# An attention and MLP block on one core: four maxima moved ahead, and K's loads, the last spare copies and a row of ones moved in the DMA queue

## The chip, the core and the metric

The kernel runs on one core of a Trainium2 chip. The core has a matrix engine (TensorE, PE in the profile, with its weight loads as PEld), a vector engine (VectorE, DVE), a scalar engine (ScalarE, ACT), a general engine (GpSimd, POOL) and a queue engine (SyncE, SP) that here issues nearly all DMAs. Each engine works through its own list of instructions in order and waits on semaphores for the others.

The metric is the device time of one execution in microseconds. Before the change it is 1146.16 us, the median of three runs (1145.81 to 1146.93).

## What is computed

One transformer block over 2048 tokens of width 448, with 16 heads of 28 columns. A conditioning vector `c` gives six modulation rows. The part that matters here is the attention, with its softmax over all 2048 keys:

```python
def _A_ref(x, wqkv, wo):
    B, S, D = x.shape
    H = 16; Dh = D // H
    qkv = (x @ wqkv).reshape(B, S, 3, H, Dh).transpose(2, 0, 3, 1, 4)
    q, k, v = qkv[0], qkv[1], qkv[2]
    scale = Dh ** -0.5
    scores = jnp.einsum("bhqd,bhkd->bhqk", q, k) * scale
    p = _softmax(scores, axis=-1)
    o = jnp.einsum("bhqk,bhkd->bhqd", p, v)
    return o.transpose(0, 2, 1, 3).reshape(B, S, D) @ wo
...
h = _layernorm(x) * (1 + ca) + sa
x = x + ga * _A_ref(h, A_wqkv, A_wo)
h = _layernorm(x) * (1 + cb) + sb
x = x + gb * _B_ref(h, B_w1, B_b1, B_w2, B_b2)
```

`_B_ref` is a second layer norm, a product with `w1`, a GELU and a product with `w2`.

## The kernel before

**Stages.** Phase 1 takes the tokens in four blocks of 512 (`b` = 0 to 3) and makes Q, K and V. Q and K are kept as a rounded high part and a low rest (`hi`, `lo`), four heads to a group (`g` = 0 to 3). `qk_task` and `v_task` are the tasks of a block; `n` counts them. Phase 2 is the attention in 16 units (a group times a block of queries) of 16 steps, and phase 3 is the MLP.

**Maxima.** The softmax needs the largest score of each query row before phase 2 can use that query block. For every group, query block, key block and head a small product (`L464`) writes 128x512 scores into a PSUM bank and VectorE reduces them to 128 maxima (`L469`). Some are done as a pair for two key blocks: ScalarE takes the positive part of the difference (`L477`) and VectorE adds and reduces in one operation (`L481`). A pair is two small products, one ScalarE and one VectorE operation; two single maxima are two products and two VectorE operations. All of them go through a ring of five PSUM banks (`ma` twice, `m2` twice, `m1`) plus the bank `o` for a sixth one. The maxima are spread over the tasks: `emit_task` puts five or six products behind each task's own product, and `emit_mid` puts four single ones into its middle. Before the change `emit_mid` is used in tasks 1, 3, 5 and 7 of block 1 alone. What is left for group 0 and query block 0 at the end of phase 1 is done by `finish_max(0, 0)`.

**The road into phase 2.** `max_fin` gathers the finished maxima of a query block (`L500`), and two tasks later `put` transposes them (`L507`) and stores them with four small DMAs (`L510`) as row 28 of each head in `slot_b`, the query tile. The first product of phase 2 (`L1155`) reads 29 rows of `slot_b` and of the key tile `slot_a`, so it waits for the four `L510`, for Q's loads and for K's loads (`L651`). K's loads of a block's 2x4 tiles go into the slots that held the weights, and read Q's and K's parts back from DRAM (`d`), where each `qk_task`'s split has stored them (`L432`, 256 KB each).

**SP's queue.** SP issues its DMAs in the order of the code. They take turns on eight semaphores, so each of them also waits until the DMA eight places before it has landed; the listing of waits shows that for every row of the queue.

- `put_spare` (`L369`) copies four heads' spare rows from DRAM to DRAM for the Q or K task before; it reads what the two `L432` of that task have written.
- `put_ones` (`L357`) writes a row of ones into a K tensor. Its source is a part of `slot_d0`. The exponentials of the first step of phase 2 (`L1160`) write into that same slot, so the first of them waits until the last `L357` has been read out.
- `L492` loads a finished group's next `hi` part, `L834` loads rows of the output weight `wo`.

In block 3, tasks 0 to 4 are Q1, K1, Q2, K2, Q3 (the last Q), and tasks 5 to 7 are V.

Of the kernel before, what the change touches and what calls it, by code (L numbers as in the profile page):

```python
# [39 lines left out]
def tile_adaln_block(ctx: ExitStack, tc: tile.TileContext, x, wqkv, wo, w1, b1, w2, b2, c, w_mod, out):  # L40
# [29 lines left out]
    def nm(t):  # L70
        uid[0] += 1
        return f"{t}_{uid[0]}"
# [22 lines left out]
    def ps_s():  # L95
        return ps_tile("pa", 2)
# [11 lines left out]
    def f(t):  # L108
        return t.bitcast(F32)
# [226 lines left out]
    def v_init(i):  # L336
        pool.memset(v_sb[i][:, :, :, DH : DH + 1], 1.0)
        pool.memset(v_sb[i][:, :, :, DH + 1 : 32], 0.0)
# [11 lines left out]
    def by_head(t):  # L350
        return t.rearrange("(j r) n -> j r n", r=32)
# [4 lines left out]
    def put_ones(g):  # L356
        sp.dma_start(  # L357
            f(dscr[1][0][g])[DH:128:32, :].rearrange("j (q r) -> j q r", r=256),
            ones[:, None, :].broadcast_to([4, 8, 256]),
        )  # L360
# [4 lines left out]
    def put_spare():  # L365
        for kind, g, sl in spare:
            n = 4 * (4 * kind + g)
            for part in range(2):
                sp.dma_start(  # L369
                    by_head(f(dscr[1][part][3]))[:, n : n + 4, sl], by_head(f(dscr[kind][part][g]))[:, DH:32, sl],  # L370
                )
        spare.clear()
# [65 lines left out]
    def v_task(b, t, p):  # L438
        ts = slice(t * 128, (t + 1) * 128)
        hh, hl = hT[b]  # L440
        mm_acc(p[:, :D], terms448(
            lambda k: hh(k)[:, ts], lambda k: hl(k)[:, ts], lambda k: wv[0][:, k, :], lambda k: wv[1][:, k, :],
        ), p1_n[3] if phase1[0] else None)
        if phase1[0]:
            emit_task(*p1_n[:3])
        act.copy(v_sb[b][:, t, :, :DH], p[:, :D].rearrange("p (h d) -> p h d", d=DH))
# [41 lines left out]
    def load_hi(kind, g, b):  # L488
        tg = ("kh" if kind else "qh") + str(b)
        t = sb.tile([128, 512], F32R, tag=tg, name=nm(tg), bufs=1)  # L490
        (kh_sb if kind else qh_sb)[(g, b)] = t
        sp.dma_start(f(t), f(dscr[kind][0][g])[:, b * 512 : (b + 1) * 512])  # L492
# [113 lines left out]
    p1_n = [0, False, 1, None]  # L606
# [41 lines left out]
    def load_parts(tag, kind, g, sl):  # L648
        t = slot(tag, [128, 2, 512])
        for part in range(2):  # L650
            sp.dma_start(f(t)[:, part, :], f(dscr[kind][part][g])[:, sl])  # L651
        return t

    def load_k(g, ch):
        kst[(g, ch)] = load_parts(f"a{ch}", 1, g, slice(ch * 512, (ch + 1) * 512))
# [37 lines left out]
    for b in range(NB):  # L693
        more = b + 1 < NB
        tasks = []
        for g in range(1 if b else 0, NG):
            tasks += [(b, 0, g), (b, 1, g)][: 2 if g + 1 < NG else 1]
        if b == 0:
            tasks[1], tasks[2] = tasks[2], tasks[1]

        tasks += [(b, 2, t) for t in range(4 if more else 3)]
        if more:
            stages, later = stages[-4:] if b else stages, ln1_stages(b + 2) if b + 2 < NB else None
            xs_next = []
            tasks += [(b + 1, 0, 0), (b + 1, 1, 0)]
        for n, (tb, kind, g) in enumerate(tasks):
            post = []
            ready, newq = newq, []
            if not more and n == len(tasks) - 2:

                mx_ring[:] = ["ma", "ma", "m2", "m2", "m1"]
            p1_n[0] = P1RATE if b < 1 else P1RATE + 1
            if not more and n == len(tasks) - 1:
                p1_n[0] = 0

            k = n - (6, 4, 4, 4)[b]
            p1_n[1] = not (more and (0 <= k < NC)) and not (b == 1 and n < 4)
            p1_n[2] = (3 if n > 3 else 1) if b == 3 else 2 if b == 2 and p1_n[1] else 1
            p1_n[3] = emit_mid if b == 1 and n in (1, 3, 5, 7) else None
            if kind < 2:  # L720
                fn = qk_task(tb, kind, g, firsts[n] if b == 0 and n < 3 else None)
                if g == 0:
                    fn()
                else:
                    post.append(fn)
                if kind == 1 and (g == 0 or (g == 1 and tb < 2)):
                    newq = [(g, qt, cch) for qt in range(tb + 1) for cch in range(tb + 1) if max(qt, cch) == tb]
            else:
                v_task(tb, g, ps_s())
            for item in ready:  # L730
                queue_max(*item)
            if b == 0 and 2 <= n < 6:
                prep_w(2, n - 2, act.copy, dve)
            if more:
                k = n - (6, 4, 4, 4)[b]

                if b == 0 and n in (0, 1, 3, 4):
                    x = 2 * n if n < 2 else 2 * n - 2
                    for fn in stages[x : x + 2]:
                        fn(xs_next)  # L740
                if b and n < 4:
                    stages[n](xs_next)
                if 0 <= k < NC:
                    post.append(h_chunk(b + 1, xs_next, k))
                if later and 7 <= n < 11:
                    later[n - 7](None)
            if n == (4 if b else 6):
                v_init(b)
            if b == 0 and n == 6:
                mod_load(0)  # L750
                mod_load(1)
            if b == 1 and n == 8:
                put_last_rows()
            if b == 2 and n == 5:
                sp.dma_start(b1_col, b1.rearrange("(k p) -> p k", p=128))
            if b == 1:
                if n < 2:
                    mod_mm(n)
                    mod_load(2 + n)
                elif n in (2, 3):  # L760
                    mod_mm(n)
                    if n == 3:
                        mod_fin()
            if not more:
                if n == 0:
                    load_q(0)
                    load_q(1)
                if n == 6:
                    put_spare()
                if n in (2, 4, 6):  # L770
                    put_ones(n // 2 - 1)
                if n == 5:
                    act.activation(cols[:, 0:1], zero_col, AF.Exp)
                    for ch in range(4):
                        load_k(0, ch)
            tick_late()
            for fn in post:
                fn()
        if more:
            stages = later  # L780
# [21 lines left out]
    phase1[0] = False  # L802
    for item in deferred:
        load_hi(*item)
    for g in range(1, NG):
        for qt in range(NB):
            for cch in range(NB):
                queue_max(g, qt, cch)
# [323 lines left out]
    for u in range(NU):  # L1132
        g, qt = divmod(u, NB)
        for kt in range(NKT):
# [10 lines left out]
            n = n_maxima(step)  # L1145
# [81 lines left out]
    for n in range(len(seq) + LAG):  # L1227
        if n < len(seq):
            b, i = seq[n]
# [53 lines left out]
```

## Time and profile before

| what | value |
|---|---|
| median of three runs | 1146.16 us |
| the profiled execution, its own time | 1145.55 us |
| its span from first to last instruction | 1143.8 us |
| granted TensorE clock, mean | 0.995 |
| PE busy in the span | 98% |
| phase 1 (PE's last product of it ends) | 167.5 us |
| phase 2's first product starts | 176.8 us |

The 1.75 us between the span and the execution's own time lie around the program. The times inside the trace are counted from the start of the span. "Idle before" in a row is time in which that engine did nothing, with the instruction or the DMA whose end let it go on.

### The profile page before, as it was taken

What the parts mean: (1) busy time and instruction counts of PE and PEld (TensorE: products, weight loads), DVE (VectorE), ACT (ScalarE), POOL (GpSimd) and SP (SyncE); (2) the same over time, 40 slices, a digit from 0 to 9 for tenths busy, and PEclk for the clock granted to TensorE, in tenths of its full rate; (3) what the DMA queues carried; (4) which work ended last, traced back from release to release, by engine and by line L of the source; (5) the groups of instructions that cost most, each with busy time, mean ns of one, the idle gap of its engine ahead of it and who ended that gap; (6) DMA issues with size and microseconds to landing.
All of it is one profiled execution on the core that took longest, in us unless ns stands there. A gap on an engine that the chain in (4) does not pass through costs nothing.

```text
span 1143.8 us, 20663 instructions
## 1 busy us (share of the span) xinstructions
PE 1125.3 (98%) x8319; PEld 674.9 (59%) x8319; DVE 832.2 (73%) x1485; ACT 672.3 (59%) x825; POOL 209.6 (18%) x211
## 2 busy tenths in 40 slices
PE   9999988999999999999999999999999999999998
PEld 6756764444444444444444444545458888888887
DVE  6968776999989999998999877586438853444322
ACT  4555755877877787877788777576862321211110
POOL 1533331210000000000000011207114503123000
PEclk9999998999999999999999999999999999999999
DMA  8562362111231211221211222020423100000000
GB/s 300 201 209 76 103 215 66 47 57 57 66 99 53 56 49 38 66 85 57 58 48 55 74 80 74 13 84 1 128 59 89 43 33 1 1 33 1 33 1 33
DMA packets 49389, 81.16 MB, mean 71 GB/s; under 512 B 12307, under 2 KB 18762, under 8 KB 49294
## 3 DMA queue, kind: packets, MB, share of 16 engines
q1 hardware_dynamic: 48810, 79.11, 21.9%
q8 instruction: 65, 1.06, 0.4%
q10 hardware_dynamic: 148, 0.46, 0.1%
q0 software_dynamic: 336, 0.28, 0.1%
q14 instruction: 30, 0.25, 0.1%
HBM read 54.94 MB, written 26.45 MB: 71 GB/s over the span
## 4 chain that ended last, share of the span: by engine, by line
PE 93%; DVE 3%; DMA 2%; issue 1%; ACT 1%; SPq 0%; POOL 0%; DVEq 0%; ACTq 0%; POOLq 0%
PE s L1155 27%; PE o L1125 21%; PE m L386 16%; PE pa L386 8%; PE m L464 6%; PE s L1218 4%; PE s L1219 4%; PE s L1217 4%; DVE mxp L469 2%; PE o L267 1%; PE m L267 1%; DMA slot_a<-d 1%; PE ma L464 0%; DMA osb<-drec 0%; DMA slot_d<-in_c_dram 0%
## 5 line engine op out<-in xcount | busy, mean ns | idle before, releaser
L469 DVE TENSOR_REDUCE mxp<-m 128x1 f32<-128x512 f32 x879 | 555.0, 684 | 97.4 <-PE m L464 94.3
L1155 PE MATMUL s<-slot_b,slot_a 28*128 28x512 f32 (+1 forms) x3072 | 384.8, 424 | 9.5 <-DMA slot_b<-full 9.2
L1160 ACT ACTIVATE slot_c<-s 128x1024 f32<-128x1024 f32 x340 | 329.6, 1022 | 82.5 <-PE s L1155 81.7
L1155 PEld LDWEIGHTS s<-slot_b,slot_a 28*128 28x128 f32 (+1 forms) x3072 | 216.9, 184 | 259.8 <-ACT slot_c L1160 148.9
L464 PE MATMUL m<-kh,qh 28*128 28x512 f32 x867 | 289.5, 472 | 0.5 <-DVE mxp L469 0.2
L1160 ACT ACTIVATE slot_d<-s 128x1024 f32<-128x1024 f32 x172 | 166.8, 1022 | 52.6 <-PE s L1155 41.4
L1125 PE MATMUL o<-slot_c,v 128*32 128x512 f32 x1360 | 181.2, 605 | 0.0
L1201 ACT ACTIVATE full<-m,b_col 128x512 f32<-128x512 f32 x56 | 38.5, 688 | 191.9 <-PE m L386 179.7
L1204 DVE CAST hi<-full 128x512 fp32r<-128x512 f32 x56 | 25.2, 450 | 135.2 <-ACT full L1201 135.2
L464 PEld LDWEIGHTS m<-kh,qh 28*128 28x128 f32 x867 | 115.0, 182 | 8.5 <-DVE mxp L469 4.8
L891 POOL TENSOR_TENSOR osb<-osb,osb 128x512 f32<-128x512 f32 x16 | 21.1, 1316 | 449.7 <-DMA osb<-drec 321.4
L1125 PE MATMUL o<-slot_d,v 128*32 128x512 f32 x688 | 92.5, 605 | 0.4 <-ACT osb L1094 0.4
L386 PE MATMUL m<-y,slot_a 128*128 128x512 f32 x160 | 60.6, 395 | 0.0
L1125 PEld LDWEIGHTS o<-slot_c,v 128*32 128x32 f32 x1360 | 26.8, 108 | 53.7 <-issue 53.3
L1205 DVE TENSOR_TENSOR lo<-full,hi 128x512 fp32r<-128x512 f32 x56 | 44.1, 788 | 5.2
L386 PE MATMUL m<-y,slot_c 128*128 128x512 f32 x152 | 47.5, 396 | 0.1
L1219 PE MATMUL s<-slot_v,lo 128*128 128x448 f32 x128 | 46.7, 365 | 0.0
L1217 PE MATMUL s<-slot_v,hi 128*128 128x448 f32 x128 | 46.6, 364 | 0.0
L469 DVE TENSOR_REDUCE mxp<-ma 128x1 f32<-128x512 f32 x56 | 36.7, 682 | 10.1 <-PE m L464 5.1
L386 PE MATMUL m<-y,slot_v 128*128 128x512 f32 x112 | 39.2, 396 | 0.0
L386 PE MATMUL m<-y,slot_b 128*128 128x512 f32 x112 | 39.0, 397 | 0.0
L477 ACT ACTIVATE slot_d<-m 128x512 f32<-128x512 f32 x33 | 18.7, 596 | 28.5 <-PE m L464 14.9
(249 smaller groups left out, 1412.1 us busy)
## 6 DMA issues: line engine op xcount, KB each, us to landing
slot_b<-d SPq DMA_DIRECT2D x32, 256.0 KB
slot_a<-d SPq DMA_DIRECT2D x32, 256.0 KB
d<-lo SPq DMA_DIRECT2D x28, 256.0 KB
d<-hi SPq DMA_DIRECT2D x16, 256.0 KB
osb<-drec SPq DMA_DIRECT2D x15, 256.0 KB
out_dram<-xn SPq DMA_DIRECT2D x16, 224.0 KB
raw<-in_B_w_dram SPq DMA_DIRECT2D x14, 224.0 KB
qh<-d SPq DMA_DIRECT2D x12, 256.0 KB
```

The lines of the kernel that those rows point to most:

```text
L386: pe.matmul(p, a, b, start=(i == 0), stop=(i == len(terms) - 1))
L464: pe.matmul(m, qh_sb[(g, qt)][js, i * 128 : (i + 1) * 128], k[js, :], start=True, stop=True)
L469: dve.tensor_reduce(out=mxp[(g, qt)][:, i, j, cch : cch + 1], in_=m, op=ALU.max, axis=AX.X)
L1125: pe.matmul(o[32 * j : 32 * j + 32, :], v_sb[kt // 4][:, kt % 4, 4 * g + j, :], p[:, j, :], start=(kt == 0), stop=(kt == NKT - 1),)
L1155: pe.matmul(s2[:, jj, :], ks[rows_, kp, kc], qs[rows_, qp, :], start=(term == 0), stop=(term == 2))
L1160: act.activation(pt[:, 2 * hf : 2 * hf + 2, :], s2, AF.Exp, scale=SCALE)
L1201: act.activation(gf, p, AF.Gelu_apprx_tanh, bias=b1_col[:, i : i + 1])
L1204: dve.tensor_copy(ghi, gf)
L1205: dve.tensor_tensor(out=glo, in0=gf, in1=f(ghi), op=ALU.subtract)
L1217: pe.matmul(pp, ghi[:, ts], w_hi, start=(m == 0), stop=False)
L1218: pe.matmul(pp, ghi[:, ts], w_lo, start=False, stop=False)
L1219: pe.matmul(pp, glo[:, ts], w_hi, start=False, stop=(m == NFT - 1))
```

## The change

Five edits, all of them in phase 1:

1. Task 8 of block 2, the last V task of that block, now has `emit_mid` in its middle: four single maxima.
2. In block 3 the tasks with three pairs begin at task 5 and no longer at task 4. Task 4 has one pair and four single maxima, as tasks 0 to 3 have.
3. K's eight loads are issued in task 4, ahead of that task's split, and no longer in task 5.
4. The last spare copies (`put_spare` of Q3) and the third row of ones (`put_ones(2)`) are issued behind phase 1, after the deferred `L492`, and no longer in task 6.
5. With edits 1 and 2 no maximum is left for `finish_max(0, 0)`; the gathering of query block 0 comes in task 4 and its store in task 5.

```diff
             p1_n[1] = not (more and (0 <= k < NC)) and not (b == 1 and n < 4)
-            p1_n[2] = (3 if n > 3 else 1) if b == 3 else 2 if b == 2 and p1_n[1] else 1
-            p1_n[3] = emit_mid if b == 1 and n in (1, 3, 5, 7) else None
+            p1_n[2] = (3 if n > 4 else 1) if b == 3 else 2 if b == 2 and p1_n[1] else 1
+            p1_n[3] = emit_mid if (b, n) in ((1, 1), (1, 3), (1, 5), (1, 7), (2, 8)) else None
...
                 if n == 0:
                     load_q(0)
                     load_q(1)
-                if n == 6:
-                    put_spare()
-                if n in (2, 4, 6):
-                    put_ones(n // 2 - 1)
+                if n == 4:
+                    for ch in range(4):
+                        load_k(0, ch)
                 if n == 5:
                     act.activation(cols[:, 0:1], zero_col, AF.Exp)
-                    for ch in range(4):
-                        load_k(0, ch)
+                if n in (2, 4):
+                    put_ones(n // 2 - 1)
...
     for item in deferred:
         load_hi(*item)
+    put_spare()
+    put_ones(2)
```

The order of the instructions shows the moves at two places. The first is SP's queue. Before, from Q2's spare copies to the first of K's loads; `d003` and `d013` are Q3's two parts in DRAM, `slot_a0` is the first key tile:

```order
L369 DMA d103_240<-d002_231 4x4x512
L369 DMA d113_244<-d012_235 4x4x512
L357 DMA d101_238<-slot_d0_4_86 4x8x256
L432 DMA d003_232<-hi_453_1905 128x512
L432 DMA d013_236<-lo_455_1907 128x512
L369 DMA d103_240<-d102_239 4x4x512
L369 DMA d113_244<-d112_243 4x4x512
L651 DMA slot_a0_463_1950<-d100_237 128x512
```

and from the last of K's loads on:

```order
L651 DMA slot_a3_466_1959<-d110_241 128x512
L369 DMA d103_240<-d003_232 4x4x512
L369 DMA d113_244<-d013_236 4x4x512
L357 DMA d102_239<-slot_d0_4_86 4x8x256
L510 DMA slot_b0_413_1740<-full_480_2024 4x4x32 x4
L492 DMA qh0_481_2038<-d001_230 128x512
L834 DMA raw_495_2097<-in_A_wo_dram 28x448 x4
```

K's first load now stands right behind Q2's two spare copies. From the last of K's loads on, the changed queue reads:

```order
L651 DMA slot_a3_464_1935<-d110_241 128x512
L357 DMA d101_238<-slot_d0_4_86 4x8x256
L432 DMA d003_232<-hi_458_1920 128x512
L432 DMA d013_236<-lo_460_1922 128x512
L369 DMA d103_240<-d102_239 4x4x512
L369 DMA d113_244<-d112_243 4x4x512
L510 DMA slot_b0_417_1752<-full_472_1977 4x4x32 x4
L492 DMA qh0_481_2035<-d001_230 128x512
L369 DMA d103_240<-d003_232 4x4x512
L369 DMA d113_244<-d013_236 4x4x512
L357 DMA d102_239<-slot_d0_4_86 4x8x256
L835 DMA raw_495_2097<-in_A_wo_dram 28x448 x4
```

Five DMAs that stood ahead of K's loads now stand between them and the maxima's four stores, and the last three small ones stand behind those stores.

The second place is PE in task 8 of block 2, the second half of its own product (`pa_376`) and the maxima behind it. Before:

```order
L386 MATMUL pa_376_1595<-slot_e1_21_126,slot_b0_221_970 128x448
L386 MATMUL pa_376_1595<-slot_e0_20_125,slot_b1_222_971 128x448 x2
L386 MATMUL pa_376_1595<-slot_e0_20_125,slot_b1h_223_972 128x448
L386 MATMUL pa_376_1595<-slot_e1_21_126,slot_b0_221_970 128x448
L386 MATMUL pa_376_1595<-slot_e0_20_125,slot_b0_221_970 128x448
L464 MATMUL m2_377_1607<-raw_159_726,qh2_276_1196 128x512
L464 MATMUL m1_378_1610<-raw_159_726,qh2_276_1196 128x512
L464 MATMUL ma_379_1613<-raw_178_806,osb_161_745 128x512
L464 MATMUL ma_380_1616<-raw_178_806,osb_161_745 128x512
L464 MATMUL m2_381_1619<-kh0_70_355,qh2_276_1196 128x512
L464 MATMUL o_382_1622<-kh0_70_355,qh2_276_1196 128x512
```

and in the changed kernel, from the first of the four new maxima on:

```order
L464 MATMUL m2_377_1601<-raw_178_806,osb_161_745 128x512
L464 MATMUL m1_378_1604<-raw_178_806,osb_161_745 128x512
L464 MATMUL ma_379_1607<-raw_178_806,osb_161_745 128x512
L464 MATMUL ma_380_1610<-raw_178_806,osb_161_745 128x512
L386 MATMUL pa_376_1595<-slot_e1_21_126,slot_b0_221_970 128x448
L386 MATMUL pa_376_1595<-slot_e0_20_125,slot_b1_222_971 128x448 x2
L386 MATMUL pa_376_1595<-slot_e0_20_125,slot_b1h_223_972 128x448
L386 MATMUL pa_376_1595<-slot_e1_21_126,slot_b0_221_970 128x448
L386 MATMUL pa_376_1595<-slot_e0_20_125,slot_b0_221_970 128x448
L464 MATMUL m2_381_1619<-raw_159_726,qh2_276_1196 128x512
L464 MATMUL m2_382_1622<-raw_159_726,qh2_276_1196 128x512
L464 MATMUL m1_383_1625<-raw_178_806,osb_161_745 128x512
```

Four of the five banks are now taken ahead of the second half, and the six maxima behind it go through the same banks once more. The numbers of PE's and VectorE's instructions in the whole program are the same in both kernels; ScalarE has two fewer.

## The prediction

> **What bounds the kernel now.** I read the page's busy times and its chain first, then the list of waits, then the timeline around the one long wait.
>
> ```profile
> span 1143.8 us, 20663 instructions
> PE 1125.3 (98%) x8319; PEld 674.9 (59%) x8319; DVE 832.2 (73%) x1485; ACT 672.3 (59%) x825; POOL 209.6 (18%) x211
> PE 93%; DVE 3%; DMA 2%; issue 1%; ACT 1%; SPq 0%; POOL 0%; DVEq 0%; ACTq 0%; POOLq 0%
> PE s L1155 <- DMA slot_b<-full: 9.2, 1, 9.2
> ```
>
> PE is busy nearly always and carries 93% of the chain. It has one wait of any size: 9.2 us, once, in which the first product of phase 2 waits for the maxima's store (`L510`, `slot_b<-full`). PE's timeline and its windows show the place:
>
> ```profile
> 166.84 0.72 PE L464 MATMUL m<-kh,qh 28*128 28x512 f32 x2
> ...
> 176.80 0.79 PE L1155 MATMUL s<-slot_b,slot_a 29*128 29x512 f32 x2 [9.24 <-DMA slot_b<-full]
> ...
> core 0: us, PE busy (x) PEld busy (x) DVE busy (x) ACT busy (x) POOL busy (x), PEclk, DMA share, GB/s
> 167.50:176.80 9.30, 0.06 (x1) 0.03 (x1) 2.78 (x6) 0.00 (x0) 0.00 (x0) 0.66 0.73 229
> 176.80:180.00 3.20, 3.20 (x18) 2.37 (x19) 2.36 (x4) 1.46 (x2) 0.45 (x1) 0.50 0.58 165
> ```
>
> Phase 1 ends at 167.56 and phase 2 begins at 176.80. All that the change can win lies in this gap, since the same products, in the same number, stand before and behind it. So I compute one moment: when the last of the four `L510` lands. It landed at 176.56, by the chain and SP's timeline:
>
> ```profile
> 160.42 1.29 SPq L369 DMA_DIRECT2D d<-d  x2
> 161.76 0.46 SPq L357 DMA_DIRECT2D d<-slot_d  x1
> 162.27 0.34 SPq L432 DMA_DIRECT2D d<-hi  x1
> 162.66 0.78 SPq L432 DMA_DIRECT2D d<-lo  x1
> 163.54 1.23 SPq L369 DMA_DIRECT2D d<-d  x2
> 164.81 4.66 SPq L651 DMA_DIRECT2D slot_a<-d  x8
> 169.51 1.67 SPq L369 DMA_DIRECT2D d<-d  x2
> 171.57 0.27 SPq L357 DMA_DIRECT2D d<-slot_d  x1
> 172.29 2.46 SPq L510 DMA_DIRECT2D slot_b<-full  x4
> 174.91 0.34 SPq L492 DMA_DIRECT2D qh<-d  x1
> ...
> 168.32 5.89 DMA slot_a<-d
> 174.23 2.33 DMA slot_b<-full
> ...
> SPq L510 <- DMA slot_a<-d: 0.4, 1, 0.4
> ```
>
> K's first load is issued at 164.81. The chain runs through one of K's loads, which lands at 174.21, to the last `L510`, whose turn on the eight semaphores it held, and 2.33 us later that has landed: 11.75 us from K's first issue. The gathering of the maxima isn't on this road: the stores wait for K's loads.
>
> **The change part by part, on that road.**
>
> *Four maxima in the middle of block 2's task 8.* The trace has this edit already in block 1, whose V tasks 6 and 7 are alike but for `emit_mid` in task 7:
>
> ```profile
> 83.39:86.87 3.48, 3.48 (x22) 2.68 (x21) 2.02 (x6) 1.53 (x3) 1.21 (x1) 1.00 0.76 292
> 86.87:92.17 5.30, 5.12 (x25) 3.21 (x24) 5.30 (x10) 3.21 (x6) 1.35 (x2) 1.00 0.21 32
> 130.81:134.26 3.45, 3.45 (x22) 2.67 (x21) 2.46 (x6) 2.32 (x5) 1.22 (x2) 1.00 0.00 0
> ...
> 90.98 1.28 DVE L469 TENSOR_REDUCE mxp<-m 128x1 f32<-128x512 f32 x2
> ...
> 91.11 0.49 PE L464 MATMUL ma<-kh,qh 28*128 28x512 f32 x1
> 91.75 0.50 PE L464 MATMUL m<-raw,osb 28*128 28x512 f32 x1
> ```
>
> Task 6 takes 3.48 us, task 7 5.30: 1.82 more. In task 7 VectorE is busy throughout, and PE's last two maxima start at 91.11 and 91.75, each right after VectorE has left its bank. Task 8 of block 2 (130.81 to 134.26) has no middle maxima yet. There too VectorE's 2.46 us are the maxima that the task before has left to it, and the fourth and fifth maxima behind it need the banks of the third and fourth middle ones. I take +1.82. The lower end is the bare products, from a middle whose banks were free:
>
> ```profile
> 60.34 0.51 PE L464 MATMUL m<-kh,qh 28*128 28x512 f32 x3
> 60.35 0.49 PE L464 MATMUL ma<-kh,qh 28*128 28x512 f32 x1
> 60.78 0.50 PE L386 MATMUL pa<-slot_c,slot_a3h 128*128 128x512 f32 x1
> ```
>
> 60.34 to 60.78 is 0.44. The upper end is VectorE's full time, four operations at half of two in 1.28 us, or 0.64 each: 2.56. What comes later in phase 1, SP's stores and loads too, hangs on these tasks and moves by the same amount.
>
> *K's loads.* Their first issue moves from 164.81 to the end of Q2's spare copies, 160.42 + 1.29 = 161.71, the start of the `L357` that it displaces at 161.76: -3.05 us. Q3's product, whose weights lie in K's slots, must be done by then, and it is; its maxima already run at
>
> ```profile
> 157.81 0.39 PE L464 MATMUL ma<-kh,qh 28*128 28x512 f32 x1
> ```
>
> The ends are -2.65, if SP waits once for a landing as the stores did (0.4), and -3.39, if the first load, with less ahead of it, comes in half a piece of 256 KB sooner (0.34, by the rate below).
>
> *What now stands between K's loads and the stores.* Before: two spare copies and a row of ones. Now the same three small ones and, new, Q3's two writes of 256 KB. The nearest price for such a piece is the rate at which K's own loads came in:
>
> ```profile
> 171.00:173.00 2.00, 0.00 (x0) 0.00 (x0) 0.00 (x0) 0.00 (x0) 0.00 (x0) 0.50 1.04 388
> ...
> 146.27 1.85 SPq L651 DMA_DIRECT2D slot_b<-d  x4
> 148.22 0.37 SPq L432 DMA_DIRECT2D d<-hi  x1
> ...
> 154.64 1.28 SPq L369 DMA_DIRECT2D d<-d  x2
> ```
>
> 262,144 bytes at 388 GB/s are 0.68 us, two are 1.35. That they would be paid is seen after Q's loads: the write issued at 148.22 behind four loads let the spare copy that reads it go only at 154.64, 6.4 us later, so pieces come through in the order of issue. The lower end is +0.55: the last store must at least wait until K's eighth load and the ones have landed instead of the seventh. The upper end is +1.65, with the small copies drawn out by 0.3 besides. I take +1.15, nearer the upper end because of that last row; part of the writes runs while the stores still wait for their turn.
>
> [...]
>
> *What is off the road.* The four maxima at the end of phase 1 (166.84, 0.72 us) go, but 9 us of waiting follow them: 0. Task 4 of block 3 gets five VectorE operations in place of three, and ScalarE two fewer. Tasks 0 to 3 have just these five:
>
> ```profile
> 144.41:147.80 3.39, 3.39 (x19) 2.46 (x17) 3.07 (x7) 1.67 (x4) 1.36 (x2) 1.00 0.45 158
> ```
>
> VectorE needs 3.07 of 3.39 us, so PE isn't held; a stall of some tenths in the shorter V task behind it ends in the gap too: 0. The store of the maxima is ready two tasks sooner, and waits for K's loads as before: 0. The last spare copies and ones behind the stores shift the loads of `wo` by about 2 us; they feed POOL, which no one waits for there: 0. The last `L357` holds back ScalarE's first exponential, whose cover is this:
>
> ```profile
> 178.54 1.94 ACT L1160 ACTIVATE slot_d<-s 128x1024 f32<-128x1024 f32 x2 [11.06 <-DMA raw<-in_A_wo_dram]
> ...
> 182.62 0.39 PE L1155 MATMUL s<-slot_b,slot_a 29*128 29x512 f32 x2
> ```
>
> PE comes back to that bank at about 182.4, behind the last V product. An exponential takes half of 1.94, so it may start as late as 181.4, 2.8 us later than now. With the stores issued at about 174.5 the `L357` follows after an `L492` (0.34), two spare copies (1.67), 0.4 of waiting and its own 0.27, at 177.2; with 2.33 to land that is 179.5: 0.
>
> *The sum.* +1.82 - 3.05 + 1.15 = -0.08. The gap shrinks at its front, to about 8 us, but its end stays: PE begins phase 2 at about 176.7. PE's clock was 0.50 in the first 3.2 us behind the gap, and I leave that as it is. The profiled execution took 1145.55 us (1143.8 and 1.75 around it), so 1145.5 by this sum. The median of the runs shown is 0.61 above that execution, so 1146.1.
>
> **The rivals.**
>
> *Faster: the lead is kept.* Block 2's task 8 finds its banks free (0.44), the writes are hidden behind the turns of the stores (0.55), and K's loads come in sooner (-3.39): -2.40, 1143.8. For it: block 2's tasks leave VectorE idle for 1 us each (2.46 of 3.45). Against it: block 1's task 6 leaves still more (2.02 of 3.48) and task 7 paid all the same. With one of the three alone it stays within 0.2%.
>
> *Slower: the ones come too late.* Place: ScalarE's first exponential behind the last `L357`. It decides from 181.4 on; from there each microsecond costs one. It is now the last of thirteen DMAs behind K's loads, where each waits for the one eight before. For it: two `L369` took 1.67 us to issue for their waits alone. Against it: 1.9 us of cover beyond my 179.5. At 184.0 it would give +2.6, 1148.7.
>
> *The change doesn't do what it says: K's loads don't go sooner.* If SP, at 161.76, still waits for landings and goes only where it went before, the lead is 0: +1.82 + 1.15 = +2.97, 1149.1; half the lead gives 1147.6. For it: SP waited at 154.64 for a write. Against it: SP went on at once, from 161.71 to 161.76, and K's first load waits for PE alone.
>
> **How the numbers follow.** The likeliest is the sum, 1146.1, with 0.58; its own range is 1144.4 to 1147.6: the middle at 0.44 alone gives -1.46, at 2.56 alone +0.66, and the runs shown lie from 0.35 below to 0.77 above their median. The kept lead has 0.18 (0.12 of it beyond 0.2%), the late ones 0.12 (0.08 beyond), the lost lead 0.12 (0.05 beyond). A difference of 0.2%, 2.3 us, is about what a measurement of this kernel can tell from no change: faster 0.12, same 0.75, slower 0.13. With a tenth left out on either side the range is 1144.0 to 1148.2.
>
> **What the changed profile would show.** Block 2's task 8 lasts about 5.3 us, and VectorE is busy through it (or 3.9, if the lead is kept). K's first load is issued near 163.6 and the last `L510` near 174.5. PE's one wait is still for `slot_b<-full`, about 8 us, and ends near 176.7; the first exponential starts before 180. If PE begins phase 2 before 175 or after 178.5, or waits for an exponential in the first two steps, the prediction is wrong; so it is if phase 2 itself is no longer as long as before.

## The result, and the profile after

The changed kernel takes 1146.44 us, the median of 12 runs (1145.59 to 1148.41); the kernel before took 1146.23 us beside it (12 runs, 1144.25 to 1148.56). The ratio is 1.0001, with a 95% interval of 0.9992 to 1.0010: no change that can be measured. The profiled execution took 1146.05 us, with a span of 1144.3. Two lines of the page, and the first of PE's list of waits:

```profile
span 1144.3 us, 20654 instructions
PE 1126.0 (98%) x8319; PEld 675.0 (59%) x8319; DVE 833.1 (73%) x1485; ACT 671.4 (59%) x823; POOL 209.8 (18%) x211
```

```profile
PE s L1156 <- DMA d<-d: 7.7, 1, 7.7
```

PE's one long wait has shrunk from 9.2 to 7.7 us. It is put down to a spare copy (`d<-d`), which the product doesn't read: that copy was landing when the wait ended, and the last `L510` had landed 0.35 us before. SP's queue after the change:

```profile
162.66 3.95 SPq L651 DMA_DIRECT2D slot_a<-d  x8
166.66 0.68 SPq L357 DMA_DIRECT2D d<-slot_d  x1
167.44 0.40 SPq L432 DMA_DIRECT2D d<-hi  x1
169.37 0.32 SPq L432 DMA_DIRECT2D d<-lo  x1
169.97 1.23 SPq L369 DMA_DIRECT2D d<-d  x2
171.33 2.62 SPq L510 DMA_DIRECT2D slot_b<-full  x4
```

In this execution all of phase 1 ran 0.92 us earlier than in the profile before, from the program's start on. So I count places from the first product of block 2's task 8, which stands at 131.22 in the profile before and at 130.30 here. K's first load moved from +33.6 to +32.4, and phase 2's start from +45.6 to +45.9. PE's timeline at that start, the first product that sums values (`o<-slot_d,v`), and ScalarE's first exponential:

```profile
176.17 0.80 PE L1156 MATMUL s<-slot_b,slot_a 29*128 29x512 f32 x2 [7.72 <-DMA d<-d]
...
178.50 4.17 PE L386 MATMUL m<-slot_e,slot_c 128*128 128x448 f32 x11
...
185.15 1.06 PE L1126 MATMUL o<-slot_d,v 128*32 128x512 f32 x8
```

```profile
178.69 1.94 ACT L1161 ACTIVATE slot_d<-s 128x1024 f32<-128x1024 f32 x2 [9.67 <-DMA raw<-in_A_wo_dram]
```

In the windows (start and end, length, PE's busy time, granted clock, DMA share, GB/s) of both kernels the gap reads like this, before first:

```profile
167.11:170.52 3.41, 0.45 (x4) 1.00 0.88 242
170.52:173.93 3.41, 0.00 (x0) 0.50 0.87 327
173.93:177.35 3.42, 0.55 (x4) 0.50 0.42 105
177.35:180.76 3.41, 3.41 (x20) 0.50 0.45 123
180.76:184.17 3.41, 3.33 (x23) 1.00 0.30 73
```

```profile
168.53:171.94 3.41, 0.00 (x0) 1.00 1.04 383
171.94:175.35 3.41, 0.00 (x0) 0.50 0.41 150
175.35:178.77 3.42, 2.60 (x17) 0.50 0.55 147
178.77:182.18 3.41, 3.41 (x10) 0.50 0.30 71
182.18:185.59 3.41, 3.09 (x24) 1.00 0.33 83
```

The clock is at half speed for 10.24 us in both, and three windows of 3.41 us, the shortest such stretch in any execution (experiment 3), tile that exactly. Before, phase 2 began 3.96 us ahead of the end of this stretch, after the change 6.01 us. So `o<-slot_d,v` comes 54.85 us behind the first product of task 8, in place of 53.60: +1.25, of which 0.29 is the later start; the 2.05 us more at half speed account for the other 1.0.

### The profile page after: what moved, and what is told of

It is laid out like the page before. It is cut to its first block, busy times and chain, and to the rows that moved or that the text cites. A ratio compares the mean times of both kernels' runs of the same rounds, so it can differ in the third digit from the quotient of the medians.

```text
span 1144.3 us, 20654 instructions
## 1 busy us (share of the span) xinstructions
PE 1126.0 (98%) x8319; PEld 675.0 (59%) x8319; DVE 833.1 (73%) x1485; ACT 671.4 (59%) x823; POOL 209.8 (18%) x211
## 4 chain that ended last, share of the span: by engine, by line
PE 94%; DVE 3%; DMA 2%; ACT 1%; issue 1%; SPq 0%; DVEq 0%; ACTq 0%
PE s L1156 27%; PE o L1126 22%; PE m L386 16%; PE pa L386 8%; PE m L464 6%; PE s L1219 4%; PE s L1220 4%; PE s L1218 4%; DVE mxp L469 2%; PE o L267 1%; DMA slot_c<-in_w_mod_dram 1%; PE ma L464 1%; PE m L267 1%; DMA slot_a<-d 0%; DMA d<-lo 0%
## 5 line engine op out<-in xcount | busy, mean ns | idle before, releaser
L464 PE MATMUL m<-kh,qh 28*128 28x512 f32 x863 | 287.4, 472 | 0.8 <-DVE mxp L469 0.5
L1161 ACT ACTIVATE slot_d<-s 128x1024 f32<-128x1024 f32 x172 | 166.8, 1022 | 51.3 <-PE s L1156 41.5
L464 PEld LDWEIGHTS m<-kh,qh 28*128 28x128 f32 x863 | 114.3, 182 | 8.6 <-DVE mxp L469 5.4
L1206 DVE TENSOR_TENSOR lo<-full,hi 128x512 fp32r<-128x512 f32 x56 | 44.1, 788 | 5.9 <-DVE hi L1205 0.9
L1218 PE MATMUL s<-slot_v,hi 128*128 128x448 f32 x128 | 46.6, 364 | 0.0
L469 DVE TENSOR_REDUCE mxp<-ma 128x1 f32<-128x512 f32 x54 | 35.6, 682 | 7.2 <-PE m L464 4.9
```

The source lines that it names most:

```text
L464: pe.matmul(m, qh_sb[(g, qt)][js, i * 128 : (i + 1) * 128], k[js, :], start=True, stop=True)
L469: dve.tensor_reduce(out=mxp[(g, qt)][:, i, j, cch : cch + 1], in_=m, op=ALU.max, axis=AX.X)
L1161: act.activation(pt[:, 2 * hf : 2 * hf + 2, :], s2, AF.Exp, scale=SCALE)
L1206: dve.tensor_tensor(out=glo, in0=gf, in1=f(ghi), op=ALU.subtract)
L1218: pe.matmul(pp, ghi[:, ts], w_hi, start=(m == 0), stop=False)
```

## The experiments

All were timed in five rounds beside the kernel before. Two tables first; "task 8" is its first product in block 2, and "half" counts the windows of 3.41 us at half clock from the gap on, by the clock record of the one profiled execution. The expectations of experiments 1, 3 and 4 count from 0.4 us earlier, from the transposes ahead of that product: their +46.3 and +32.8 are 45.9 and 32.4 here. The first table rests on one execution of each kernel. That of experiment 6 was its fastest (1141.95 us), those of experiments 7 and 9 were their slowest (1142.86 and 1148.39), and that of experiment 1 its second slowest (1150.38).

| kernel | K's first load, from task 8 | phase 2 starts | distance | PE's wait | half |
|---|---|---|---|---|---|
| before | 33.6 | 45.6 | 12.0 | 9.2 | 3 |
| changed | 32.4 | 45.9 | 13.5 | 7.7 | 3 |
| 1 changed, no middle maxima | 30.8 | 45.8 | 15.1 | 9.9 | 5 |
| 2 changed, writes behind the stores | 32.0 | 43.4 | 11.4 | 5.3 | 2 |
| 3 changed, 30 idle products | 32.4 | 46.6 | 14.2 | 1.8 | 1 |
| 4 changed, V product in the gap | 32.1 | 46.3 | 14.2 | 5.9 | 5 |
| 5 before, middle maxima | 35.6 | 47.7 | 12.1 | 9.3 | 3 |
| 6 changed, road clear | 32.3 | 42.4 | 10.2 | 4.3 | 2 |
| 7 three edits, 24 idle products | 30.4 | 41.5 | - | 0 | 1 |
| 8 changed, ones later | 33.2 | 46.5 | 13.3 | 8.4 | 3 |
| 9 three edits mended, 20 idle products | 30.4 | 42.3 | 11.8 | 1.7 | 5 |
| 10 as 1, once more | 30.5 | 44.1 | 13.6 | 8.1 | 4 |
| 11 as 9, no idle products | 30.3 | 41.2 | 10.8 | 5.1 | 3 |
| 12 as 9, 24 idle products, ones from an idle tile | 29.7 | 41.5 | - | 0 | 0 |

| kernel | median, us | ratio to before | 95% interval |
|---|---|---|---|
| 1 | 1147.52 | 1.0013 | 1.0003 to 1.0023 |
| 2 | 1144.20 | 0.9990 | 0.9980 to 1.0001 |
| 3 | 1145.56 | 0.9992 | 0.9983 to 1.0000 |
| 4 | 1147.33 | 1.0005 | 0.9997 to 1.0014 |
| 5 | 1147.71 | 1.0011 | 1.0002 to 1.0020 |
| 6 | 1143.64 | 0.9980 | 0.9972 to 0.9989 |
| 7 | 1141.00 | 0.9954 | 0.9942 to 0.9967 |
| 8 | 1146.47 | 1.0002 | 0.9993 to 1.0011 |
| 9 | 1143.66 | 0.9977 | 0.9966 to 0.9987 |
| 10 | 1147.75 | 1.0010 | 1.0001 to 1.0019 |
| 11 | 1145.34 | 0.9989 | 0.9981 to 0.9998 |
| 12 | 1142.35 | 0.9962 | 0.9950 to 0.9974 |

**The four middle maxima (experiments 1, 5 and 10).** Experiments 1 and 10 are the same kernel, the changed one without them; experiment 5 is the kernel before with them alone.

```diff
-            p1_n[3] = emit_mid if (b, n) in ((1, 1), (1, 3), (1, 5), (1, 7), (2, 8)) else None
+            p1_n[3] = emit_mid if b == 1 and n in (1, 3, 5, 7) else None
```

> The changed kernel without the four maxima in the middle of block 2's task 8; the pairs that this leaves are done by the later tasks of block 3, and nothing is left behind the phase. All places are counted from the start of block 2's task 8, where the changed kernel's first product of phase 2 starts at +46.3 us and its first K load is issued at +32.8. Theory (phase 2's start hangs on K's loads and the stores behind them, and the four maxima cost 1.82 us because VectorE holds their banks): task 8 takes 3.45 us again, K's loads go at +30.95, phase 2 starts at +44.5, PE's wait stays at about 7.7 us, and the time falls by 1.8 us, to about 1144.6. Rival (the start hangs on the maxima, which now end two tasks later): phase 2 stays at +46.3, PE's wait grows to 9.5 us, time unchanged.

> The kernel before with one edit: the four maxima in the middle of block 2's task 8. Counted from that task's first product, K's first load is issued at +33.6 us in the kernel before and phase 2 starts at +45.6. Theory A (what the prediction said: everything behind the task moves by what the four maxima cost): task 8 takes 1.83 us more, K's first load goes at +35.4, phase 2 starts at +47.4, and the time is 1.8 us longer, 1148.0. Rival B (taking the four maxima out of the changed kernel sent K's loads 1.6 us sooner and brought phase 2 no nearer, so the end of the loads doesn't follow their issue one for one): phase 2 starts at +45.6 to +46.3, and the time is at most 0.7 us longer.

> The changed kernel without the four maxima in block 2's task 8, the same kernel as in the first experiment, once more. There K's first load was issued 1.6 us sooner than in the changed kernel and phase 2 started no sooner (15.1 us from the one to the other, where four kernels with the same transfers behind K's loads show 13.3 to 14.2). Theory (chance: single packets of 2 KB stalled for up to 2 us in that execution): the distance is 13.3 to 14.3 us this time, phase 2 starts at +44.1 to +45.0. Rival (the loads meet the writes of K2 that are still under way when they are issued sooner): the distance is 15 us again, phase 2 at +45.8. In both, phase 1 ends 2.2 us sooner, so that one more window of 3.41 us may be at half speed: time 1145 to 1147.5.

In experiment 1, K's loads went 1.6 us sooner than in the changed kernel, and phase 2 started no sooner. Had that been a rule, the price of the middle maxima would not have counted. Experiment 5 says that it is none: phase 2 starts at +47.7, 2.1 us later than before (1.83 of task 8, 0.16 more ahead of K's loads and 0.11 behind them), and the time rises by 1.2 us. Phase 2's first product in its PE timeline, where task 8 begins at 130.97:

```profile
178.65 0.79 PE L1155 MATMUL s<-slot_b,slot_a 29*128 29x512 f32 x2 [9.32 <-DMA slot_b<-full]
```

Experiment 10 confirms it: 13.6 us from K's first load to phase 2, as in the other kernels with these transfers, and a start at +44.1, 1.8 us sooner than in the changed kernel. So the 15.1 us of experiment 1 don't come back with the same kernel, and the theory of chance stands. Its trace shows where they arose, though not in packets of 2 KB, the longest of which took 1.4 us. SP's fourth issue of K's loads took 2.35 us where most take 0.43; in the chain of work that ended last it reads:

```profile
162.50 2.35 SPq L651
```

In the same time, from 162.54 on, one packet of 8 KB on the queue that the profile calls `instruction` took 2.17 us. Experiments 9 and 10 have the like, an issue of 1.55 and 1.48 us beside such a packet of 1.47 and 1.10 us. That the issue waits for the packet isn't shown.

But experiments 1 and 10 took 1.1 and 1.3 us longer than the changed kernel by their medians, though PE began phase 2 as early or earlier. One reason is that the four maxima aren't saved, and that block 3's tasks don't do all that is left over, as the expectation said. Of the 1024 small products of the program, the kernels without middle maxima do 205 in phase 1 and 819 in phase 2, the kernel before and the changed one 209 and 815. What the listing of `L464` shows for phase 2, the changed kernel first, then experiment 10:

```profile
L464 PE MATMUL m<-kh,qh x815: 382/492/791, 176.2 to 781.3; 28*128 28x512 f32 x163
L464 PE MATMUL m<-kh,qh x819: 383/494/792, 174.7 to 782.8; 28*128 28x512 f32 x164
```

Three of the four are in its first steps. In the three steps that begin with the second group of `o<-slot,v` products PE takes 8.22 us in place of 7.08, with two more of the small products and the clock full in both. In experiment 5 phase 2 has 811, which fits that a start later by 2.1 us cost only 1.2. The other reason is the clock, in experiment 10's windows of PE:

```profile
177.88:181.29 3.41, 3.41 (x10) 0.50 0.24 66
181.29:184.70 3.41, 2.87 (x23) 1.00 0.28 82
184.70:188.12 3.42, 3.42 (x24) 0.50 0.09 28
```

PE waits 0.54 us for VectorE's maxima in step 1 (0.32 in the changed kernel), where VectorE has six in a row in place of five; the window with that wait holds 2.87 us of work, and the window behind it is at half speed once more. In experiments 1 and 11, which have no middle maxima either, the same stands there: 2.87 us of work, then a window at half speed. In the kernel before and in experiments 2, 5, 6 and 8 and the changed kernel the corresponding window holds 3.09 to 3.33 us, and full speed stays. Of the lead of 1.8 us with which experiment 10 begins phase 2, 0.7 is gone by the first `o<-slot_d,v`, 1.1 goes in the step with that window and 1.1 in the three steps behind it: 1.2 us behind the changed kernel, about what the times show. Experiments 7, 9, 11 and 12 have the same 819 products and pay for them too.

**What stands between K's loads and the stores (experiments 2 and 6).** Experiment 2 holds Q3's two writes back until the stores and the last ones are issued; experiment 6 holds back the second row of ones and the last spare copies too.

```diff
+            if (kind, g, b) == (0, NG - 1, NB - 1):
+                last_write.append(write)
...
         load_hi(*item)
+    put_ones(2)
+    last_write[0]()
     put_spare()
-    put_ones(2)
```

> The changed kernel with the two writes of Q3's last split behind the stores of the maxima and behind the last row of ones. In the changed kernel 13.5 us lie between K's first load and PE's restart. Theory (the writes stand in the queue ahead of the stores and are paid, 1.15 to 1.4 us): this distance falls to 12.1 to 12.4 us and PE's wait from 7.7 to about 6.4. Because the clock stays at half speed until about 182.2 whenever PE resumes, only half of it reaches the end: 0.6 us, to about 1145.8. Rival (each DMA takes its own time, whatever is queued): distance 13.5, wait 7.7, time unchanged.

> The changed kernel with nothing between K's eight loads and the four stores of the maxima: Q3's two writes, the second row of ones and the last spare copies all stand behind the stores, the ones first. From K's first load to phase 2 are 13.5 us in the changed kernel, 12.0 in the kernel before, 11.4 with the two writes alone behind the stores. Theory (each small copy, too, delays the stores): 10.0 to 10.8 us, phase 2 at +42.5 to +43.2 from block 2's task 8, time about 1143.7. Rival (the small copies are free, only the 512 KB of writes counted): 11.4 us, +43.6, time as with the writes alone, 1144.2.

In experiment 6 the last row of ones is issued ahead of the last spare copies and overwrites a row that they read, so that one row of four heads' keys is wrong; the number and size of the transfers are the same. SP's queue and the start of phase 2, experiment 2 first:

```profile
162.47 4.30 SPq L658 DMA_DIRECT2D slot_a<-d  x8
167.26 0.26 SPq L357 DMA_DIRECT2D d<-slot_d  x1
167.94 1.77 SPq L370 DMA_DIRECT2D d<-d  x2
170.04 2.45 SPq L517 DMA_DIRECT2D slot_b<-full  x4
```

```profile
173.87 0.79 PE L1164 MATMUL s<-slot_b,slot_a 29*128 29x512 f32 x2 [5.26 <-DMA slot_b<-full]
```

and experiment 6:

```profile
162.81 4.41 SPq L658 DMA_DIRECT2D slot_a<-d  x8
168.11 2.44 SPq L517 DMA_DIRECT2D slot_b<-full  x4
```

```profile
172.96 0.79 PE L1165 MATMUL s<-slot_b,slot_a 29*128 29x512 f32 x2 [4.35 <-DMA slot_b<-full]
```

The writes ahead of the stores are paid: 13.3 to 14.2 us with everything ahead of the stores (the changed kernel, experiments 3, 4, 8 and 10; 15.1 in experiment 1), 11.4 without the writes. So they cost some 2.3 us, more than the forecast of 1.15 to 1.4 and than the 1.35 us that their bytes make at the rate of K's loads, and the rival by which each DMA takes its own time, whatever is queued, falls. Whether it is their bytes or their two turns on the eight semaphores (SP waits 1.5 us ahead of the second write for one of K's loads to land) wasn't separated.

The price of the small copies isn't shown. Experiment 6 has 10.2 us, 1.2 less, where their 96 KB make 0.25 at the rate of K's loads. But experiments 9 and 11, where nothing stands between K's loads and the stores either, have 11.8 and 10.8. By the records of semaphores the last store lands 10.0 to 11.7 us behind K's first load in the five executions with a clear road (10.7 in three of them), and 11.3 us in experiment 2. In time experiment 6 gains 2.3 us over the kernel before, and experiment 2 1.1, with an interval that takes in no change.

**The clock behind the gap (experiments 3 and 4).** Experiment 3 lets PE do 30 products on old data behind phase 1; experiment 4 does the last V product there instead of in step 0.

```diff
     finish_max(0, 0)
     tick_late(True)
+    pd = ps_s()
+    for _ in range(30):
+        pe.matmul(pd, hT[NB - 1][0](0)[:, 0:128], hT[NB - 1][0](1), start=True, stop=True)
+    act.copy(sbt("full", [128, 512], bufs=3), pd)
```

```diff
     tick_late(True)
+    v_task(NB - 1, 3, ps_s())
...
             if step == 0:
-                v_task(NB - 1, 3, ps_mx())
                 emit_max(2)
```

> The changed kernel with 30 products of 128x512 more, on old data, right behind phase 1, whose result nobody uses (some 6.6 us of PE in the gap of 7.7). Theory (the half-speed stretch of 10.24 us is a consequence of PE's idleness in the gap): the clock stays at full speed, phase 2 starts where it did (+46.3 us from block 2's task 8), the 6 us at half speed behind it cost 2.5 to 3 us less, and the time falls by as much, to about 1143.7. Rival 1 (the drop has another cause, such as the transfers in the gap): the half-speed stretch stays, time unchanged. Rival 2 (the first exponential, waiting for the ones until 178.5, becomes the limit at once): the clock is full, but PE waits for exponentials in the first two steps and the gain is under 1 us.

> The changed kernel with the last V product (11 products of 128x448, some 2.0 us at full speed, 4.17 us in the changed kernel's first step at half speed) done right behind phase 1, in the gap, instead of in step 0 of phase 2. Theory (a half-speed stretch of exactly 10.24 us begins some 3 us behind the end of phase 1's last product): phase 2 starts at the same place, +46.3, with PE's wait 5.7 us; the stretch begins and ends 2 us later, so that 8 us instead of 6 behind the restart are at half speed; net 2.0 less work minus 1.0 us lost: about 1 us faster, 1145.4. Rival (the stretch ends a fixed time after PE resumes, or where it ended before): 2 to 3 us faster. Second rival (the V product was the cover of the first exponential): PE waits for exponentials in step 1, no gain.

Experiment 3's windows:

```profile
171.89:175.31 3.42, 3.26 (x15) 1.00 0.42 156
175.31:178.72 3.41, 1.70 (x16) 1.00 0.53 128
178.72:182.13 3.41, 3.31 (x9) 0.50 0.38 97
182.13:185.55 3.42, 3.11 (x25) 1.00 0.37 88
```

The transfers in the gap are the same (a DMA share of 1.05 in its first window, 1.04 in the changed kernel's) and the clock is at 1.00 through it, where it was at 0.50, so PE's idleness is what drops it here. The stores landed late here (14.2 us), PE waited 1.8 us, and the window with that wait (1.70 us of PE work) was followed by one at half speed. In 5 of the 11 timed runs the clock was full all through; their median is 1144.4, 2 us below the changed kernel. PE waited for no exponential in these steps, so rival 2 falls. The theory holds, with less of a gain than it said.

My theory of a stretch of exactly 10.24 us fell with experiment 2, whose stretch took 6.83 us and ended at 180.45, where its expectation had about 182.2, and with experiment 4, whose windows are

```profile
174.84:178.25 3.41, 0.20 (x4) 0.50 0.37 95
178.25:181.67 3.42, 3.41 (x18) 0.50 0.30 80
181.67:185.08 3.41, 3.28 (x19) 0.50 0.31 79
185.08:188.49 3.41, 3.41 (x24) 0.50 0.39 103
188.49:191.91 3.42, 3.42 (x24) 0.50 0.06 15
```

Five windows are at half speed, although PE is busy in the last four, and the time is no shorter (1147.33 us, where 1145.4 was forecast). PE waited for exponentials for 0.3 us in the whole span, so the second rival falls as well. In eleven of the thirteen executions with such a stretch full speed was back behind one or two busy windows (3.16 to 3.42 us of PE work). I first thought that the big V product does it, which experiment 4 had taken out of step 0; but experiment 9 has it there and stayed at half for five windows too. What a window must hold to bring full speed back stays open.

**The last row of ones (experiment 8).** It is issued behind the first four of `wo`'s loads.

```diff
     put_spare()
-    put_ones(2)
...
                 sp.dma_start(r[32 * j : 32 * j + DH, :D], wo[DH * hd : DH * hd + DH, :])
+            if g == 0:
+                put_ones(2)
```

> The changed kernel with the last row of ones behind the first four of wo's loads, so that it is issued some 2.2 us later and lands at about 180.7 instead of 178.5. ScalarE's first exponential waits for it. The prediction gave that exponential cover until 181.4 and costed its delay at nothing. Theory: the exponential starts at about 180.7, 4.5 us behind the start of phase 2 instead of 2.5, PE waits for it nowhere, time unchanged (1146.4). Rival (the cover is gone, since phase 2 starts sooner than reckoned): PE waits for an exponential in step 1 and the time is 1 to 2 us longer.

ScalarE's timeline and, for 165 us to 200, PE's list of waits:

```profile
181.08 1.94 ACT L1162 ACTIVATE slot_d<-s 128x1024 f32<-128x1024 f32 x2 [11.97 <-DMA d<-slot_d]
```

```profile
PE s L1157 <- DMA d<-d: 8.4, 1, 8.4
PE m L464 <- DVE mxp L469: 0.3, 1, 0.3
```

The first exponential starts 4.1 us behind phase 2's start instead of 2.5, PE waits for none, and the time is that of the changed kernel. The cover is there.

**All together (experiments 7, 9, 11 and 12).** No middle maxima, the road clear as in experiment 6, and idle products behind phase 1. Experiment 7 has the wrong row of experiment 6; in the others the spare copies of K2 go ahead of the last ones.

> The changed kernel with three edits at once: the stores directly behind K's loads (as in the run before this), no four maxima in the middle of block 2's task 8, and 24 products on old data (5.6 us) behind phase 1 whose result nobody uses. Theory (the stores end 10 to 11 us behind K's first load, which now goes at +30.8, so that phase 2 starts at about +41.5, right behind the idle products at +41.8, and the clock stays full): about 4.5 us less than before, 1141.6. Rival (the loads don't land sooner for being issued sooner): phase 2 at +43 to +43.5, PE waits 1.5 us, one window of 3.41 us at half speed, about 1143.

> The run with three edits again, with two differences: the last spare copies of K's second group stand ahead of the last row of ones, which overwrites a row that they read, and 20 idle products instead of 24, since the stores had landed about 0.8 us before the 24 were through. Everything is computed. Theory: phase 2 starts at +40.7 (0.7 to 0.8 us sooner than with 24), PE's wait is under 0.5 us, at most one window at half speed, time 1140.5 to 1141. Rival (the last row of ones, now behind two more copies and the writes, holds the first exponential past PE's need): a wait for ScalarE in step 1, time 1142 or more.

> As the run with 20 idle products, but without them. Theory (their whole gain is the clock, and the stores end where they do with them): phase 2 starts at +40.7, PE's wait is 4.5 us, two or three windows are at half speed, and the time is 1.5 to 3 us longer than with the products, 1142.5 to 1143.5. Rival (the clock behind the gap costs nothing, since ScalarE and the transfers set phase 2's first steps): same time as with the products, within 0.5 us.

> The mended run of three edits with 24 idle products again, and with the rows of ones copied from a tile that ScalarE doesn't write (an idle tile of the layer norm), so that the first exponential waits for no row of ones. Everything is computed. Theory (what the mended run lost was the first exponential's wait for the last row of ones, 4.4 us behind the start of phase 2, and PE's idle time ahead of it): phase 2 starts at +41.5 to +42, the first exponential about 1.8 us behind it, at most one window at half speed in most runs, time 1141 to 1142. Rival (it lost by PE's wait for the stores alone): exponential sooner, time still about 1143.5.

Experiment 7 came out at 1141.00 us (5 runs), near its forecast of 1141.6. Experiment 9 missed its forecast by 3 us: the last store went out 1.1 us later than in experiment 7 by the records of single packets, 20 products left PE waiting 1.7 us, and the first exponential waited for the ones until 4.4 us behind phase 2's start. Four of its 12 runs had the full clock throughout; their median is 1142.35. Experiment 11, without the idle products, is slower than experiment 9 by 1.7 us (1.5 to 3 were forecast), though in the profiled executions its phase 2 starts 1.1 us sooner: what the products bring is the clock (0.998 in the median of experiment 9's runs, 0.996 in experiment 11's). Experiment 12 repairs both faults of experiment 9: 24 products again, and the ones copied from a tile that ScalarE doesn't write.

```diff
+                    ones2.append(xn_t()[0:4, 0:256])
+                    pool.memset(ones2[0], 1.0)
...
-            ones[:, None, :].broadcast_to([4, 8, 256]),
+            ones2[0][:, None, :].broadcast_to([4, 8, 256]),
```

Its PE timeline has no wait in the gap:

```profile
166.73 5.63 PE L798 MATMUL pa<-slot_c 128*128 128x512 f32 x24
172.29 0.50 PE L1175 MATMUL s<-slot_b,slot_a 29*128 29x512 f32 x2
...
174.21 2.50 PE L388 MATMUL m<-slot_e,slot_c 128*128 128x448 f32 x11
...
179.54 1.06 PE L1145 MATMUL o<-slot_d,v 128*32 128x512 f32 x8
```

The V product of step 0 takes 2.50 us in place of 4.17, and `o<-slot_d,v` comes 7.3 us behind phase 2's start in place of 9.0. The time is 1142.35 us (6 runs, 1141.30 to 1142.72), just above its forecast of 1141 to 1142 and 0.38% below the kernel before (0.26% to 0.50%); the changed kernel's ratio to that one is 1.0001. Which of experiment 9's two faults cost it more wasn't separated: its four runs at full clock took as long as experiment 12, with both faults in. No run has the clear road and the idle products with the middle maxima kept.

## Why the prediction was right

The forecast was 1146.1 us with no change as the likeliest; measured are 1146.44 and a ratio of 1.0001. By its own steps:

- **Four middle maxima, +1.82.** Right: task 8 took 5.28 us in place of 3.45, VectorE busy throughout, and PE's fourth and fifth maxima behind it started late.

```profile
129.89:135.17 5.28, 5.11 (x26) 3.22 (x25) 5.28 (x10) 3.25 (x7) 1.41 (x2) 1.00 0.00 0
```

  That it moves all behind it is shown by experiments 5 and 10.
- **K's loads, -3.05.** Right: counted from task 8 their first issue moved by -1.23, which is +1.82 - 3.05.
- **Q3's writes between the loads and the stores, +1.15.** The mechanism was right, the size too small: five executions with this order show 13.3 to 14.2 us, on average 13.75 (14.0 with experiment 1's 15.1), against 12.0 and 12.1, so +1.7, just over the upper end of 1.65. The price taken, two pieces at the rate of K's loads, was too low: taken away, the writes gave back some 2.3.
- **The sum, -0.08.** With +1.7 it is +0.5. Phase 2 started 0.3 us later in the changed kernel and 0.7 to 1.1 later in experiments 3, 4 and 8: below what the time can tell.
- **Off the road, 0.** Right for the first exponential: it started at 178.69, its wait cost nothing, and experiment 8 shows 1.6 us more that cost nothing. For the four end maxima, task 4 and the earlier gathering the profile shows no wait; no run took them alone.
- **The clock behind the gap, left as it is.** Right in the count of windows (three and three), but by luck, since the prediction gave no reason for it, and the other executions show none to five. Nor is it without weight: in the profiled execution it took 0.96 us behind the gap, and in experiment 3 the idle products, which do nothing but hold the clock up, gained 0.9 us by the medians, although its phase 2 starts 0.8 us later.

Of the rivals, the kept lead fell with task 8's 5.28 us and with experiment 5. The ones that come too late fell with experiment 8. That K's loads don't go sooner fell with their issue. The signs named came as said, the 0.92 us of the earlier start taken off: K's first load at 163.6, the last store's issue done at 174.9, the wait near 8 us and over at 177.1 by that count (176.7 was said), the exponential before 180. The name in PE's list of waits differs, and phase 2 is not quite as long as before, which the prediction had named as a sign of being wrong: from its start to the end of the span it takes 968.1 us in place of 967.0, and 0.96 of that lies in the stretch at half speed.

## What to carry to other kernels

Here the wait for the last link of a chain of DMAs grew with what stood ahead of it in the queue (13.3 to 14.2 us from K's first load to phase 2 with Q3's writes ahead of the stores, 11.4 without): put what somebody waits for first, then the rows that ScalarE needs freed, and writes that nobody awaits last. Work taken out of one stage turns up in another: count it there, and ask whether that stage has room, as phase 2, bound by PE, had not for four small products. And when a wait of TensorE is shortened, look at the clock in the steps behind it before reckoning with the gain: in experiment 10 a wait of half a microsecond was followed by a window at half speed that cost 1.1 us, and in experiment 9 idle products through the gap were worth more than a start 1.1 us sooner.

## What the runs showed of the hardware

**The stretches at half speed were multiples of 3.41 us.** Every one around the gap, in the thirteen profiled executions that have one, is such a multiple: 3.41, 6.83, 10.24, 13.65 or 17.07. They begin at other places of the program in each execution: 39.3 us behind task 8's first product in the kernel before, 41.6 in the changed one. The windows are counted from the edges of these stretches. A window at full speed with 0.0 to 1.73 us of PE work was followed by one at half speed there, but for experiment 2's, whose 1.81 us were nearly all a V product; windows with 2.39 to 2.69 us at the end of phase 1 (experiments 5, 10 and 11) were not either. In phase 2's mix of products one with 2.86 or 2.87 us was so in four executions (experiments 1, 7, 10 and 11), and none with 3.09 or more. Part of the scatter between runs of one kernel goes with the clock: in experiment 2 seven runs with a mean clock of 0.997 took 1142.8 to 1145.1 us, and the one at 0.993 took 1149.49; one window at half speed is 0.0015 of the mean clock. But not all of it: the changed kernel's fastest and slowest run, 1145.59 and 1148.41 us, both have 0.996.

**Not every busy window brings full speed back.** In eleven executions one or two windows at half speed with 3.16 to 3.42 us of PE work stood ahead of full speed; in experiments 4 and 9 it took four and five, with PE busy for 3.06 to 3.42 us of each. No run tells why.

**K's first loads came in slower than the later ones, in three kernels.** The last stretches of phase 1 and the gap, in the changed kernel's windows of all engines:

```profile
164.00:166.00 2.00, 2.00 (x14) 1.25 (x12) 0.98 (x5) 1.97 (x4) 0.00 (x0) 1.00 0.95 225
166.00:168.00 2.00, 2.00 (x13) 1.86 (x11) 1.55 (x5) 1.82 (x4) 0.00 (x0) 1.00 0.87 167
168.00:170.00 2.00, 0.45 (x3) 0.07 (x1) 0.37 (x2) 0.53 (x1) 0.00 (x0) 1.00 1.00 371
170.00:172.00 2.00, 0.00 (x0) 0.00 (x0) 0.00 (x0) 0.00 (x0) 0.00 (x0) 0.99 1.03 378
```

With the DMA share near 1 they move 167 and 225 GB/s at first and 371 to 378 later. The kernel before moved 202 GB/s from 167.0 to 168.5 and 388 from 171.0 to 173.0, experiment 2 193 and 202 from 164 to 168 and 370 from 168 to 170. The records show single packets of 2 KB there that took up to 1.6 us, in experiment 4 up to 2.4, where the median is 84 ns. The kernel before, where the longest took 1.1 us, and all the experiments have some of 0.8 us or more. What they wait for stays open.
